# The first quarter of W_in at the head of the load queue, in a fused decay-attention and gated-MLP kernel

## The chip, the cores and the metric

The kernel runs on one core of a Trainium2 chip. The metric is the device time of one execution in microseconds (us), from repeated runs; a profiled execution, taken by the hardware profiler, gives the trace. Five engines work beside each other, each through its own instructions in order: PE (matrix products; its weight loads are shown apart as PEld), DVE and ACT (elementwise work, and copies out of PSUM, where PE writes), POOL (elementwise work in SBUF) and SP, which here only issues DMAs. The DMAs of a core share 16 DMA engines.

## The reference, cut to what matters

Two parts follow each other. First a linear attention with decay over 4 batches, 8 heads, 768 positions and head size 64, in blocks of 64 with a running state; then a gated MLP with a mixing over positions.

```python
for b in range(nb):                                     # blocks of 64 positions
    intra = np.einsum('bhic,bhjc->bhij', qb, kb) * Dmask[None]
    intra = np.einsum('bhij,bhjd->bhid', intra, vb)
    inter = np.einsum('bhid,bhde->bhie', qb * lam_pow[None], kv_state)
    out[:, :, sl] = intra + inter
    kv_state = lam_block[None, :, None, None] * kv_state + np.einsum('bhsd,bhse->bhde', kb_dec, vb)
...
h = np.maximum(x @ w_in, 0.0)                           # x: 4 x 768 x 512, w_in: 512 x 1024
u, v = h[..., :512], h[..., 512:]
v_n = (v - mu) / np.sqrt(var + 1e-06)
v_s = np.einsum('ts,bsd->btd', w_spatial, v_n) + b_spatial[None, :, None]
return (u * v_s) @ w_out
```

## The kernel before

The positions are worked in 12 steps of 256, three to a batch. A step loads 512 KB each of q, k and v (`load`, L193: per partition 8 heads of 2 positions, 512 bytes in a piece), multiplies q and k by powers of the decay and casts them to bf16 (`decay`, L328: `QM` and `KM`, on POOL or DVE), transposes them on PE (`TQ`, `TK`, L363), copies the transposes out of PSUM (`EQ`, `EK`), forms the scores on PE (`SC`, L393), masks them on DVE (`MK`, L398), and builds the output (`AV`, L456 and L465) and the state (`KP`, L422). The output, as `xT`, goes through W_in (`PV`, L490, the half v; `PU`, L541, the half u), then normalisation, the mixing over positions (`PW`, L567), the gate (`GM`, L573) and W_out (`PO`, L578).

Inputs arrive in float32 and pass through staging tiles. W_in comes in four quarters of 512 KB through `w_h` (L250): `WH.0` and `WH.1` are the two halves by rows of the columns for v, both in `wst_0`, with 2 KB in a piece; `WH.2` and `WH.3` are the columns for u, in `wst_1`. `CW.0` and `CW.1` cast the two row groups of `WH.0` to bf16, on POOL; `CW.2` and `CW.3` cast those of `WH.1`, on DVE. The first `PV` needs all four. There are three buffers each for q, k and v, so the loads of steps 0 to 2 wait for no buffer.

Before the first data, PE runs matmuls on a tile of ones (`FL`, L306) that no result uses.

Nothing schedules: a table written out by hand, `ORDER`, is the program. Each token names an operation, its arguments and, last, its engine (S is SP, P POOL, D DVE, A ACT, T PE); each engine runs its own tokens in the order of the table, and semaphores make it wait for data. `LK.n`, `LQ.n` and `LV.n` are the loads of step n, all on SP, one behind the other; so are the quarters of W_in and later the weights of the mixing (`WQ`, L271), W_out (`WP`, L280) and the stores (`ST`, L601).

Of the kernel before, what the change touches and what calls it, by code (L numbers as in the profile page):

```python
# [13 lines left out]


ORDER = """
lam.A BR.A tab.0.A LK.0.S LQ.0.S LV.0.S LQ.1.S LK.1.S LK.2.S LV.1.S LQ.2.S WH.0.S WH.1.S posk.P idn.P msk.P one.D
row.D FL.1.512.1.1.T FL.1.512.2.1.T FL.1.512.3.1.T LB.6.T FL.1.512.5.1.T FL.1.512.4.1.T FL.1.512.1.1.T FL.1.512.2.1.T
FL.1.512.3.1.T FL.1.512.4.1.T FL.1.512.1.1.T FL.1.512.5.1.T FL.1.512.2.1.T LN.6.A LL.D mkc.D LX.A QM.0.0.P TQ.0.0.1.T
KM.0.0.D KM.0.1.D QM.0.1.P TK.0.0.0.T TK.0.1.4.T TQ.0.1.3.T EK.0.0.0.D QM.1.0.D QM.1.1.D EQ.0.0.1.A EK.0.1.4.A VC.0.P  # L20
# [620 lines left out]
```

## Time and profile before

| | |
|---|---|
| time, median of 2 runs | 141.23 us (141.09 to 141.37) |
| time of the profiled execution | 141.1 us |
| its span, first to last instruction | 139.4 us |
| mean granted TensorE clock in the span | 0.983 |
| moved by DMA | 34.12 MB, mean 245 GB/s |
| read from and written to HBM | 24.38 MB, 6.29 MB |

The span is what the trace covers; the 1.7 us between it and the time lie around it. A share of busy time is a mean over the whole span, and the stages of a step have different limits, so the views are read by stretches of time. The time to landing in the list of DMA issues runs from the issue to the last byte, with whatever stands in front of it in the queue. Line numbers (L193 and so on) are those of the code above. An idle time in brackets is that of the engine just before the instruction, with what ended it.

### The profile page before, as it was taken

The numbers are of one execution on the slowest core, as the hardware profiler recorded it, in microseconds if no ns is written. First come the engines' busy times: TensorE is split into PE (matmuls) and PEld (weight loads), VectorE is DVE, ScalarE is ACT, GpSimd is POOL, SyncE is SP. The second block draws the span as 40 slices with busy tenths as digits, with TensorE's granted clock in tenths as the row PEclk, the third lists the DMA queues.
The fourth block names the chain that finished last, engine by engine and source line by source line (L and its number), as shares of the span: only waits on it lengthen the run. The fifth ranks groups of instructions, "written<-read, shape, count | busy, mean of one in ns | idle before, by whom it ended". The sixth has DMA issues, their size and how long they took to land.

```text
span 139.4 us, 4677 instructions
## 1 busy us (share of the span) xinstructions
PE 131.3 (94%) x1964; PEld 83.6 (60%) x1978; DVE 114.7 (82%) x235; ACT 76.2 (55%) x148; POOL 60.2 (43%) x70
## 2 busy tenths in 40 slices
PE   5889989999999999999999999999999999999990
PEld 2256755687766666658666466685565665756530
DVE  1549998999997989799788978999799699985470
ACT  3156468799733588659412177782313649790101
POOL 5168654942987458900942059907702000000000
PEclk9996899999999999999999999999999999999998
DMA  3999999999999899997941899999736540025285
GB/s 89 348 346 348 387 362 363 391 382 349 366 345 307 254 315 310 301 206 214 331 106 40 209 353 361 352 228 258 123 75 80 209 172 5 0 98 203 105 304 196
DMA packets 56729, 34.12 MB, mean 245 GB/s; under 512 B 13827, under 2 KB 51971, under 8 KB 56708
## 3 DMA queue, kind: packets, MB, share of 16 engines
q1 hardware_dynamic: 56560, 33.69, 83.5%
q8 instruction: 15, 0.25, 0.7%
q10 hardware_dynamic: 148, 0.13, 0.3%
q14 instruction: 6, 0.05, 0.1%
HBM read 24.38 MB, written 6.29 MB: 220 GB/s over the span
## 4 chain that ended last, share of the span: by engine, by line
PE 84%; DMA 4%; SPq 3%; DVE 3%; issue 2%; POOL 1%; ACT 0%; DVEq 0%; POOLq 0%
PE ps L567 23%; PE ps L541 15%; PE ps L490 15%; PE ps L578 14%; DMA k_in<-in_k_dram 4%; PE ps L393 4%; PE ps L465 4%; SPq L193 3%; PE ps L363 2%; PE ps L456 2%; PE ps L422 2%; POOL kc L328 1%; PE ps L553 1%; DVE qc L328 1%; PE ps L587 1%
## 5 line engine op out<-in xcount | busy, mean ns | idle before, releaser
L567 PE MATMUL ps<-wt_sb,vn 128*128 128x384 bf16 x192 | 33.1, 326 | 0.0
L398 DVE TENSOR_TENSOR a_sb<-ps,m 128x1024 bf16<-128x1024 f32 x24 | 28.6, 1215 | 2.3 <-PE ps L393 1.2
L328 POOL TENSOR_TENSOR kc<-k_in,lv 128x512 bf16<-128x512 f32 x22 | 22.5, 1042 | 14.7 <-PE ps L422 5.2
L567 PEld LDWEIGHTS <-vn 128*128 128x128 bf16 x192 | 18.4, 98 | 11.8
L541 PE MATMUL ps<-xT,win_sb 128*128 128x256 bf16 x192 | 23.5, 273 | 0.0
L328 POOL TENSOR_TENSOR qc<-q_in,lqn 128x512 bf16<-128x512 f32 x20 | 20.8, 1057 | 5.6 <-DMA q_in<-in_q_dram 5.5
L490 PE MATMUL ps<-win_sb,xT 128*128 128x512 bf16 x89 | 22.0, 379 | 0.5 <-issue 0.2
L578 PE MATMUL ps<-wout_sb,gT 128*128 128x512 bf16 x85 | 21.2, 380 | 0.4
L541 PEld LDWEIGHTS <-win_sb 128*128 128x128 bf16 x192 | 18.2, 98 | 3.9 <-DVE xT L180 0.2
L573 DVE TENSOR_TENSOR gT<-ps,uT 128x384 bf16<-128x384 f32 x32 | 16.7, 551 | 4.1 <-PE ps L567 4.0
L178 ACT ACTIVATE o_sb<-ps 128x512 f32<-128x512 f32 (+1 forms) x14 | 7.6, 565 | 16.6 <-PE ps L578 10.4
L505 DVE BATCH_NORM_STATS2 st<-vh 128x6 f32<-128x512 bf16 x24 | 16.3, 679 | 0.1
L182 POOL CAST vb<-v_in 128x1024 bf16<-128x1024 f32 (+1 forms) x10 | 9.9, 995 | 12.8 <-PE ps L465 6.7
L178 ACT ACTIVATE ps<-bsp 128x384 f32<-128x384 f32 x23 | 10.9, 487 | 7.2 <-DVE gT L573 5.2
L490 PEld LDWEIGHTS <-xT 128*128 128x128 bf16 x96 | 8.8, 98 | 9.8 <-ACT xT L178 1.5
L578 PEld LDWEIGHTS <-gT 128*128 128x128 bf16 x92 | 8.7, 98 | 9.3
L495 ACT ACTIVATE vh<-ps 128x512 bf16<-128x512 f32 x19 | 11.1, 597 | 5.8 <-PE ps L490 5.4
L178 ACT ACTIVATE xT<-ps 128x512 bf16<-128x512 f32 x20 | 11.1, 593 | 5.2 <-PE ps L465 4.4
L180 DVE COPY o_sb<-ps 128x512 f32<-128x512 f32 x11 | 7.6, 688 | 3.9 <-PE ps L578 3.3
L495 ACT ACTIVATE uT<-ps 128x512 bf16<-128x512 f32 x17 | 9.8, 591 | 1.4 <-PE ps L541 1.3
L393 PE MATMUL ps<-qT,kT 64*64 64x128 bf16 x384 | 10.1, 226 | 0.1
L465 PE MATMUL ps<-a_sb,vb 64*64 64x128 bf16 x384 | 10.2, 221 | 0.0
(78 smaller groups left out, 159.0 us busy)
## 6 DMA issues: line engine op xcount, KB each, us to landing
k_in<-in_k_dram SPq DMA_DIRECT2D x12, 512.0 KB, 6.3
q_in<-in_q_dram SPq DMA_DIRECT2D x12, 512.0 KB, 6.3
v_in<-in_v_dram SPq DMA_DIRECT2D x12, 512.0 KB, 6.7
out_dram<-o_sb SPq DMA_DIRECT2D x23, 256.0 KB, 2.4
wst<-in_moe_w_in_dram SPq DMA_DIRECT2D x4, 512.0 KB, 7.7
wst<-in_moe_w_spatial_dram SPq DMA_DIRECT2D x4, 384.0 KB, 5.5
wst<-in_moe_w_out_dram SPq DMA_DIRECT2D x1, 1024.0 KB
wss<-in_moe_w_spatial_dram SPq DMA_DIRECT2D x2, 384.0 KB, 6.0
```

The lines of the kernel that those rows point to most:

```text
L178: nc.scalar.activation(out=o, in_=i, func=AF.Copy)
L328: vec(e).tensor_tensor(out=dst[n % NCA][:, u].rearrange("p u m o d -> p o (u m) d"), in0=src[n % NIN].rearrange("p (o u) m d -> p o u m d" ...
L393: nc.tensor.matmul(out=pa[o][row(c), w, j], lhsT=kT[n % NTR][row(o), u, j, c * Q64:(c + 1) * Q64], rhs=qv(n, o, u, c), start=(w == 0 and j ...
L398: nc.vector.tensor_tensor(out=a_sb[n % NA][:, i].rearrange("p o w j x -> p o w (j x)"), in0=ps[:, b0:b1 + 1:b1 - b0].rearrange("p o (w y) ...
L465: nc.tensor.matmul(out=po[c ^ o][row(w), c, i], lhsT=vb[n % NCA][row(c), 4 * o + u, j, :], rhs=a[row(c), i, o, w, j, :], start=(r == 0 and ...
L490: nc.tensor.matmul(out=bank(b), lhsT=x[:, slot(c, g)], rhs=win_sb[:, g, DH:DFF], start=(g == 0), stop=(g == NCH - 1))
L495: nc.scalar.activation(out=o, in_=i, func=AF.Relu)
L505: nc.vector.bn_stats(out=st6[p2][:, t], in_=vh[p2][:, t])
L541: nc.tensor.matmul(out=pu[:, f2].rearrange("p (c x) -> p c x", c=2), lhsT=win_sb[:, g, f * P:(f + 1) * P], rhs=x[:, slot(0, g):slot(1, g) ...
L567: nc.tensor.matmul(out=bank(b)[:, 0:HW], lhsT=vn[bb % 2][:, s, f * P:(f + 1) * P], rhs=wt_sb[:, s, i * HW:(i + 1) * HW], start=False, stop ...
L573: nc.vector.tensor_tensor(out=gT[bb % 2][:, f, cols], in0=bank(b)[:, 0:HW], in1=uT[bb % 2][:, f, cols], op=ALU.mult)
L578: nc.tensor.matmul(out=bank(b), lhsT=gT[bb % 2][:, f, t * P:(t + 1) * P], rhs=wout_sb[:, f, :], start=(f == 0), stop=(f == NCH - 1))
```

## The change

One token of `ORDER` moves: `WH.0.S`, the load of the first quarter of W_in, from behind `LQ.2.S`, where it is the ninth load of SP's queue, to the front of it, ahead of `LK.0.S`.

```diff
-lam.A BR.A tab.0.A LK.0.S LQ.0.S LV.0.S LQ.1.S LK.1.S LK.2.S LV.1.S LQ.2.S WH.0.S WH.1.S posk.P idn.P msk.P one.D
+lam.A BR.A tab.0.A WH.0.S LK.0.S LQ.0.S LV.0.S LQ.1.S LK.1.S LK.2.S LV.1.S LQ.2.S WH.1.S posk.P idn.P msk.P one.D
```

The instructions of SP, at the head of its queue. In the names, the first digit is the buffer (here also the step), the last number is the tile's own; behind them stands the shape of the transfer:

```order
@@ -1,3 +1,4 @@
 L636 UNCONDITIONAL_BRANCH
+L250 DMA wst_0_141<-in_moe_w_in_dram 128x2x512
 L193 DMA k_in_0_93<-in_k_dram 128x8x128
 L193 DMA q_in_0_90<-in_q_dram 128x8x128
```

The quarter now stands ahead of k of step 0, and k, q and v of step 0 and all behind them move one place back. Further down the same queue, at the old place:

```order
 L193 DMA v_in_1_97<-in_v_dram 128x8x128
 L193 DMA q_in_2_92<-in_q_dram 128x8x128
-L250 DMA wst_0_141<-in_moe_w_in_dram 128x2x512 x2
+L250 DMA wst_0_141<-in_moe_w_in_dram 128x2x512
 L193 DMA v_in_2_98<-in_v_dram 128x8x128
 L250 DMA wst_1_142<-in_moe_w_in_dram 128x4x256
```

Of the two quarters that stood behind q of step 2 one is left there, and from it on every load has its old place. On PE, DVE, ACT and POOL the instructions and their order are the same before and after. On POOL, these rows use the loads of steps 0 to 2 and then the moved quarter (the last row):

```order
L328 TENSOR_TENSOR qc_0_101<-q_in_0_90,lqn_71 128x2x4x64 x2
L182 CAST vb_0_103<-v_in_0_96 128x1024
L328 TENSOR_TENSOR kc_1_100<-k_in_1_94,lv_70 128x2x4x64 x2
L328 TENSOR_TENSOR kc_0_99<-k_in_2_95,lv_70 128x2x4x64 x2
L182 CAST vb_1_104<-v_in_1_97 128x512
L328 TENSOR_TENSOR qc_0_101<-q_in_2_92,lqn_71 128x2x4x64
L182 CAST win_sb_84<-wst_0_141 128x512 x2
```

Neither their order nor their number moved; the casts of the quarter still stand behind the decay of q of step 2.

## The prediction

> **What bounds the kernel now.** I read the busy times first, then the same by stretches, then the chain of work that ended last, and for the start of that chain the order of time on single engines and on the DMA queue. The page's head, and a view of busy time in three stretches (columns: the stretch, its length, busy us and count of PE, PEld, DVE, ACT and POOL, then the granted TensorE clock, the DMA share and GB/s):
>
> ```profile
> span 139.4 us, 4677 instructions
> PE 131.3 (94%) x1964; PEld 83.6 (60%) x1978; DVE 114.7 (82%) x235; ACT 76.2 (55%) x148; POOL 60.2 (43%) x70
> 0.00:20.00 20.00, 16.40 (x315) 9.95 (x316) 13.37 (x26) 9.80 (x21) 12.18 (x21) 0.91 0.99 312
> 20.00:130.00 110.00, 109.09 (x1620) 70.78 (x1633) 97.13 (x204) 65.00 (x125) 48.00 (x49) 1.00 0.84 234
> ```
>
> From 20 us to 130 us PE shows no work in only 110.00 - 109.09 = 0.91 us. What starts late at 20 us therefore ends late: there is almost no idle time in which PE could catch up. Before 20 us PE is busy 16.40 us of 20, so something else sets the pace there. The chain in order of time (start, length, what) says what:
>
> ```profile
> 0.80 0.46 SPq L193
> ...
> 3.25 1.45 SPq L193
> 4.74 6.00 DMA k_in<-in_k_dram
> ...
> 10.87 2.05 POOL kc L328 x2
> ...
> 16.88 1.34 DVE qc L328
> ...
> 19.27 0.64 PE ps L393 x32
> 19.91 1.19 PE ps L490 x5
> ```
>
> The chain begins on the queue of loads: issues on SP, then the transfer of k of step 1, and only then engines. From 19.27 us it is PE. The order of time on DVE and POOL in that stage (in brackets the idle time before, and who ended it):
>
> ```profile
> 4.77 1.29 DVE L328 TENSOR_TENSOR kc<-k_in,lv 128x512 bf16<-128x512 f32 x2 [0.37 <-DMA k_in<-in_k_dram]
> 9.24 1.29 DVE L328 TENSOR_TENSOR qc<-q_in,lqn 128x512 bf16<-128x512 f32 x2 [0.74 <-DMA q_in<-in_q_dram]
> 10.45 2.46 DVE L398 TENSOR_TENSOR a_sb<-ps,m 128x1024 bf16<-128x1024 f32 x2
> 14.27 1.23 DVE L398 TENSOR_TENSOR a_sb<-ps,m 128x1024 bf16<-128x1024 f32 x1 [0.23 <-PE ps L393]
> 16.88 1.34 DVE L328 TENSOR_TENSOR qc<-q_in,lqn 128x512 bf16<-128x512 f32 x1
> 6.32 2.04 POOL L328 TENSOR_TENSOR qc<-q_in,lqn 128x512 bf16<-128x512 f32 x2 [3.34 <-DMA q_in<-in_q_dram]
> 10.87 4.05 POOL L328 TENSOR_TENSOR kc<-k_in,lv 128x512 bf16<-128x512 f32 x4 [1.53 <-DMA k_in<-in_k_dram]
> 16.63 1.04 POOL L328 TENSOR_TENSOR qc<-q_in,lqn 128x512 bf16<-128x512 f32 x1 [1.15 <-DMA q_in<-in_q_dram]
> 17.81 1.44 POOL L182 CAST win_sb<-wst 128x512 bf16<-128x512 f32 x2
> ```
>
> Five waits end with a load: k0 at 4.77, q0 at 6.32, q1 at 9.24, k1 at 10.87 and q2 at 16.63 us (the digit is the step). DVE, once it has q1, works with little pause up to 18.22 us. So the first stage is set by when the first eight loads land, and they land in the order in which SP issues them. Of that queue, the rate and the beginnings (the GB/s rows have 40 slices of the stretch named: first 0 to 4.7 us, then the totals of 4.7 to 6.5 and of 16.3 to 16.9 us, then the slices of 77.7 to 79.7 and of 108 to 110 us):
>
> ```profile
> GB/s 0 0 0 0 0 0 0 0 0 0 0 0 0 0 0 0 61 113 113 118 96 118 122 179 183 288 336 353 349 340 362 336 357 336 349 349 344 344 353 344
> DMA packets 1235, 0.62 MB, mean 347 GB/s; under 512 B 16, under 2 KB 1235, under 8 KB 1235
> DMA packets 121, 0.25 MB, mean 413 GB/s; under 512 B 0, under 2 KB 0, under 8 KB 121
> GB/s 0 31 51 82 51 41 41 51 92 20 20 31 41 82 102 113 133 174 195 123 123 123 143 143 225 266 297 297 338 338 348 328 338 389 369 328 348 338 348 328
> GB/s 0 0 0 0 287 205 451 410 369 492 287 492 492 287 451 410 369 205 41 0 0 0 0 0 0 0 0 0 0 0 0 0 0 0 0 0 0 0 0 0
> k_in<-in_k_dram SPq DMA_DIRECT2D x1, 512.0 KB, 3.9
> ```
>
> The q, k and v loads move in packets of 512 bytes, at 347 GB/s once under way: 512 KB (0.524 MB) take 1.51 us. W_in moves in packets of 2 KB, in the trace at 413 GB/s: a quarter, also 512 KB, takes 1.27 us. The first load does not begin at full rate.
>
> **The change part by part.** Removed: one DMA issue between q2 and the second quarter (rows of SP below). Added: the same DMA at the head of the queue. No instruction of PE, DVE, ACT or POOL changes or changes place.
>
> ```profile
> 9.21 1.45 SPq L193 DMA_DIRECT2D q_in<-in_q_dram  x1
> 10.70 2.00 SPq L250 DMA_DIRECT2D wst<-in_moe_w_in_dram  x2
> ```
>
> (1) What the eight loads lose. All of k0, q0, v0, q1, k1, k2, v1 and q2 now stand behind one more transfer of 512 KB. If it cost what a load costs, they would land 1.51 us later; at its own rate 1.27 us. But part of it falls into time that the queue now wastes. In the first row of GB/s the slices are 0.1175 us long; the eleven from 61 to 336 sum to 1727, where 347 in each would be 3817. The missing 2090 x 0.1175 us is 0.246 MB, which is 0.71 us at 347 GB/s. After a pause at 77.7 us a 512-byte load begins just as slowly (31 to 195 GB/s for the first 19 slices of 0.05 us), while a store with 2 KB packets, at 108 us, is at 287 in its first slice and about 400 at once. If the quarter began like that store and filled all of the slow beginning, the loads would lose 1.27 - 0.71 = 0.56 us. So the bounds are 0.56 and 1.51 us. The store's row is the nearest in packet size, though it is no load; and k0's own slow beginning would run mostly beside the quarter's transfer. I take 0.85 us, nearer the lower end, which is 0.42 of the 0.71 us won back.
>
> The Trainium skill, "DMA: Bandwidth & Descriptors", Specifications, gives 512 B as the smallest transfer for line rate. By that alone the quarter would cost what a load costs, 1.51 us, and the sum would be 142.6 us; the rows of 347 and 413 GB/s differ from it. That sum is rival B below.
>
> (2) What the later loads lose: nothing. The ninth place is empty now, so the second quarter stands behind the same bytes as before, and everything behind it too. Of the five waits listed none belongs to a load behind it.
>
> (3) What the quarter's early landing wins: nothing. It is used by the two casts on POOL at 17.81 us, which have no bracket: they begin when the decay of q2 (16.63 + 1.04 us) is done, and that waits for q2. POOL reaches them 0.85 us later than before. The other two casts, on DVE, also stand behind its work of this stage.
>
> (4) What of the 0.85 us is lost again before 19.27 us. On POOL nothing can be made up: its waits for k1 and q2 move with the loads. On DVE the stretch from q1 to 18.22 us has one wait for PE, 0.23 us at 14.27 us, which could shrink. A further reason for it stands in the clock (stretches as above):
>
> ```profile
> 8.40:11.82 3.42, 3.40 (x77) 1.96 (x78) 2.67 (x5) 2.03 (x5) 1.89 (x2) 1.00 1.15 346
> 11.82:15.23 3.41, 3.24 (x64) 2.53 (x62) 3.15 (x6) 2.26 (x5) 3.41 (x5) 0.50 1.14 355
> 15.23:18.64 3.41, 2.91 (x100) 2.05 (x100) 3.41 (x6) 1.72 (x4) 2.12 (x4) 1.00 1.09 382
> ```
>
> PE has half its clock from 11.82 to 15.23 us; work that slides past 15.23 us would run at full clock, if that stretch stays where it is. The gain is bounded by that wait: 0 to 0.23 us. I take 0, because the stretch may move with the load.
>
> (5) PE's pause. The filler matmuls on ones need no load and end when they did; the first transposes come later:
>
> ```profile
> 3.44 2.86 PE L306 MATMUL ps<-ones 128*128 128x512 bf16 x9
> 7.42 0.40 PE L363 MATMUL ps<-ident,qc 128*128 128x128 bf16 x4 [1.12 <-POOL qc L328]
> ```
>
> The pause of 1.12 us grows to 1.97 us. Nothing is lost by the pause itself beyond (1).
>
> Sum: the profiled execution took 141.1 us, its span 139.4 us and 1.7 us around it. 141.1 + 0.85 (1) + 0 (2) + 0 (3) - 0 (4) = 141.95, said as 142.0 us. The median of the two runs, 141.23 us, is 0.13 us above that execution, well inside what I can price.
>
> **The rivals.** A: the forecast, a delay of about 0.6 to 1.1 us that passes through whole, 141.7 to 142.2 us. For it: five waits on loads, a stage that ends on PE at 19.27 us, and 0.91 us of idle PE in the 110 us behind.
>
> B: the quarter costs a full slot, 1.2 to 1.5 us: 142.3 to 142.6 us. For it: the slow beginning may belong to the first load from a queue at rest, of whatever packet; the 2 KB row is a store. Against it: packets that are four times as large ought to bring four times the bytes at the same count.
>
> C: the delay is hidden or made up, 141.0 to 141.4 us. For it: 0.56 us less the 0.23 us of DVE's wait is 0.33 us, and a little of the 0.91 us of idle PE could go too. Against it: DVE and POOL both hang on loads before 17 us.
>
> D, the other side of 2%: TensorE's clock stays at half for one stretch more, 15.23 to 18.64 us, since PE has less work in the time before. In that stretch it is busy 2.91 us at full clock and would need up to 2.91 us more, which gives 141.95 + 2.91 = 144.9 us at most. It decides (over 2%, that is over 144.05 us) from 2.1 us of these 2.91 that reach the end. Against it: DVE is busy all of that stretch (3.41 of 3.41 us), so it hides much of a slower PE, and the half-clock stretch itself was left after 3.41 us with PE busy 3.24.
>
> The Trainium skill, "TensorE: Matmul & The Clock Gate", Part 1, has the clock halved after an idle window of about 3.4 us. By that rule a pause of 1.97 us changes nothing and D would give 141.95 us like A. The trace agrees in the length, 3.41 us, but not in the cause: the half clock came after a stretch in which PE was busy 3.40 of 3.42 us. So D keeps a chance.
>
> **How the numbers follow.** A 0.55, B 0.20, C 0.14, D 0.11 (half of it over 2%). The time is A's, 142.0 us. The range must leave out no more than 2 in 10: from 141.2, within C (half of C left out, 0.07), to 143.0 us, which holds B and the smaller part of D (about 0.08 left out). A alone has 141.7 to 142.2. About 2% is what a measurement of this kernel can tell from no change, so a slowdown of 0.6% counts as the same. Faster by over 2% would need a gain, and no part shows one: 0.01. Slower by over 2% is half of D: 0.06. The same: 0.93.
>
> **What would show it.** In the trace after: DVE's first decay of k0 at about 5.6 us instead of 4.77, q1's at about 10.1 instead of 9.24, POOL's k1 at 11.7 instead of 10.87, q2's at 17.5 instead of 16.63; the casts of W_in on POOL without a wait, at 18.7; the scores of step 2 on PE at about 20.1 instead of 19.27. In the first GB/s slices no row near 113. From 20 us on every stage the same length. B shows as 1.2 us or more at the same places; C as a shift at 5 us that is gone at 20 us; D as a clock of 0.50 behind 15.23 us. The prediction is wrong if the first loads land no later, or if a stage behind 20 us changes its length by more than some tenths of a us.

## The result, and the profile after

The changed kernel takes 145.46 us (median of 2 runs, 145.33 to 145.58) where the kernel before takes 141.23: the ratio is 1.0266, 95% interval 1.0208 to 1.0324. A second measurement, of six runs beside seventeen of the kernel before, gave 146.16 us against 141.52, ratio 1.0327 (1.0283 to 1.0372). It is slower by some 4.2 to 4.6 us, and lies above the predicted range. One slow run, of e10 below (145.96 us), is left out of the medians and ratios.

The head of the page after, and busy time by stretches (columns as before):

```profile
span 143.9 us, 4677 instructions
PE 134.6 (94%) x1964; PEld 85.4 (59%) x1978; DVE 114.2 (79%) x235; ACT 76.2 (53%) x148; POOL 60.3 (42%) x70
0.00:20.00 20.00, 15.57 (x163) 8.34 (x164) 8.29 (x17) 6.80 (x14) 11.38 (x21) 0.76 0.96 283
20.00:130.00 110.00, 108.84 (x1745) 71.47 (x1759) 99.62 (x208) 67.85 (x131) 48.96 (x50) 1.00 0.84 233
```

PE has done 163 matmuls by 20 us where it had done 315, and DVE 8.29 us of work instead of 13.37; the mean clock of that stretch is 0.76 instead of 0.91. Behind it nothing changed. The first product with W_in, in the kernel before and then after:

```profile
19.84 3.63 PE L490 MATMUL ps<-win_sb,xT 128*128 128x512 bf16 x15
```

```profile
24.29 3.63 PE L490 MATMUL ps<-win_sb,xT 128*128 128x512 bf16 x15
```

From its start to the end of the span it is 139.4 - 19.84 = 119.56 us before and 143.9 - 24.29 = 119.61 us after. The whole difference, 4.45 us, is there at this product. How it comes about stands in the order of time on DVE and POOL after:

```profile
7.31 1.29 DVE L328 TENSOR_TENSOR kc<-k_in,lv 128x512 bf16<-128x512 f32 x2 [2.91 <-DMA k_in<-in_k_dram]
11.81 1.29 DVE L328 TENSOR_TENSOR qc<-q_in,lqn 128x512 bf16<-128x512 f32 x2 [0.77 <-DMA q_in<-in_q_dram]
13.02 1.22 DVE L398 TENSOR_TENSOR a_sb<-ps,m 128x1024 bf16<-128x1024 f32 x1
16.55 1.23 DVE L398 TENSOR_TENSOR a_sb<-ps,m 128x1024 bf16<-128x1024 f32 x1 [2.31 <-PE ps L393]
19.27 1.23 DVE L398 TENSOR_TENSOR a_sb<-ps,m 128x1024 bf16<-128x1024 f32 x1 [0.49 <-PE ps L393]
21.87 0.68 DVE L328 TENSOR_TENSOR qc<-q_in,lqn 128x512 bf16<-128x512 f32 x1
24.47 2.36 DVE L398 TENSOR_TENSOR a_sb<-ps,m 128x1024 bf16<-128x1024 f32 x2
8.86 2.04 POOL L328 TENSOR_TENSOR qc<-q_in,lqn 128x512 bf16<-128x512 f32 x2 [5.89 <-DMA q_in<-in_q_dram]
13.71 4.04 POOL L328 TENSOR_TENSOR kc<-k_in,lv 128x512 bf16<-128x512 f32 x4 [1.83 <-DMA k_in<-in_k_dram]
18.27 1.04 POOL L328 TENSOR_TENSOR qc<-q_in,lqn 128x512 bf16<-128x512 f32 x1
19.25 1.16 POOL L182 CAST win_sb<-wst 128x512 bf16<-128x512 f32 x2
```

Two parts can be read off. First, the loads: k0, q0 and q1 are used 2.54, 2.54 and 2.57 us later (4.77, 6.32 and 9.24 us before). Second, a longer stage: from q1's use to the masks of step 2 (the last DVE row; 20.14 us before) it is 12.66 us instead of 10.90, so 1.76 us more. In it DVE waits for scores of PE, 2.31 and 0.49 us, where before it waited 0.23. These waits grew by 2.57 us, more than the stage; DVE's other rows became shorter, above all its decay of q2, 0.68 us instead of 1.34. POOL reaches its own part of q2 at 18.27 us and, unlike before (16.63), does not wait for the load there. Why PE is late, in stretches of its clock, and in its order of time (the bias matmuls of L292 were 0.91 us a pair before):

```profile
7.03:10.44 3.41, 0.76 (x10) 0.49 (x10) 1.29 (x2) 0.05 (x1) 1.58 (x2) 1.00 1.13 337
10.44:20.68 10.24, 9.97 (x149) 6.40 (x147) 6.50 (x11) 4.81 (x10) 8.14 (x10) 0.50 1.06 323
```

```profile
3.44 3.87 PE L306 MATMUL ps<-ones 128*128 128x512 bf16 x9
9.96 0.40 PE L363 MATMUL ps<-ident,qc 128*128 128x128 bf16 x4 [2.65 <-POOL qc L328]
...
12.06 1.64 PE L292 MATMUL ps<-bsp,one_row 1*128 1x384 f32 x2
13.63 0.64 PE L422 MATMUL ps<-vb,kc 64*64 64x64 bf16 x32
14.21 1.64 PE L292 MATMUL ps<-bsp,one_row 1*128 1x384 f32 x2
15.78 0.64 PE L393 MATMUL ps<-qT,kT 64*64 64x128 bf16 x16
```

PE's pause is 2.65 us instead of 1.12, and its clock is halved from 10.44 to 20.68 us, 10.24 us instead of 3.41. The two pairs of bias matmuls stand in PE's order between the first and the second half of step 0's scores; at half clock they take 1.64 us each instead of 0.91, and the second half of the scores, for which DVE's second mask waits, starts only at 15.78. The chain of waits now runs through them:

```profile
1.82 6.89 DMA q_in<-in_q_dram
...
12.13 1.57 PE ps L292 x2
13.70 0.57 PE ps L422 x26
14.28 1.57 PE ps L292 x2
15.85 0.57 PE ps L393 x14
```

And the slow beginning of the queue did not go; GB/s in slices of 0.1175 us from 0 to 4.7 us:

```profile
GB/s 0 0 0 0 0 0 0 0 0 0 0 0 0 0 0 0 139 52 70 17 105 401 314 296 227 139 209 192 244 261 366 292 314 218 183 140 209 301 296 327
DMA packets 476, 0.62 MB, mean 133 GB/s; under 512 B 15, under 2 KB 224, under 8 KB 476
```

In 4.7 us 0.62 MB were moved where the kernel before had moved 0.73 MB. With W_in at the head the queue is slower, not faster, and slow until about 4.5 us.

### The profile page after: what moved, and what is told of

The parts are those of the page before. It is cut to its first block, busy times and chain, and to the rows that moved or that the text cites. A ratio compares the mean times of both kernels' runs of the same rounds, so it can differ in the third digit from the quotient of the medians.

```text
span 143.9 us, 4677 instructions
## 1 busy us (share of the span) xinstructions
PE 134.6 (94%) x1964; PEld 85.4 (59%) x1978; DVE 114.2 (79%) x235; ACT 76.2 (53%) x148; POOL 60.3 (42%) x70
## 4 chain that ended last, share of the span: by engine, by line
PE 82%; DVE 6%; DMA 5%; issue 2%; ACT 1%; POOL 1%; SPq 1%; DVEq 0%; POOLq 0%
PE ps L567 22%; PE ps L541 15%; PE ps L578 14%; PE ps L490 12%; DMA q_in<-in_q_dram 5%; PE ps L393 5%; PE ps L363 3%; PE ps L465 3%; DVE a_sb L398 2%; PE ps L456 2%; PE ps L292 2%; PE ps L422 2%; PE ps L553 1%; DVE win_sb L180 1%; DVE s_sb L437 1%
## 5 line engine op out<-in xcount | busy, mean ns | idle before, releaser
L398 DVE TENSOR_TENSOR a_sb<-ps,m 128x1024 bf16<-128x1024 f32 x24 | 28.6, 1217 | 4.7 <-PE ps L393 3.7
L393 PE MATMUL ps<-qT,kT 64*64 64x128 bf16 x384 | 10.6, 234 | 0.3 <-ACT kT L178 0.3
L178 ACT ACTIVATE qT<-ps 128x512 bf16<-128x512 bf16 (+1 forms) x7 | 5.4, 776 | 9.9 <-PE ps L363 9.9
```

Of the source, the lines that this page charges most:

```text
L178: nc.scalar.activation(out=o, in_=i, func=AF.Copy)
L393: nc.tensor.matmul(out=pa[o][row(c), w, j], lhsT=kT[n % NTR][row(o), u, j, c * Q64:(c + 1) * Q64], rhs=qv(n, o, u, c), start=(w == 0 and j ...
L398: nc.vector.tensor_tensor(out=a_sb[n % NA][:, i].rearrange("p o w j x -> p o w (j x)"), in0=ps[:, b0:b1 + 1:b1 - b0].rearrange("p o (w y) ...
```

## The experiments

The theory after the first result had two parts. L: the loads come 2.5 us late, and that passes to the end. C: PE's half-clock stretch is longer because PE pauses longer, and that costs the other 1.8 us, through DVE's wait for scores. The rivals are that the clock costs nothing, that its stretches are chance, or that the quarter's bytes disturb something else.

This table holds, for each run, when k0 is first used, PE's pause ahead of its first transpose, how long the granted clock is 0.50 in the first 25 us, the stage from q1's use to the masks of step 2, and the time (the median, with the ratio to the kernel before where it was repeated; otherwise one time, beside 141.06 us for the kernel before in e5 to e8 and 141.26 in e13 and e14). All but the times come from one trace each. Between traces with the same loads, k0's first use varies by 0.2 to 0.3 us (4.77 to 4.96 us with k0 first, 7.01 to 7.31 with the quarter first), so smaller differences mean nothing.

| run | k0 used | pause | half clock | stage | time |
|---|---|---|---|---|---|
| before | 4.77 | 1.12 | 3.41 | 10.90 | 141.23 |
| changed | 7.31 | 2.65 | 10.24 | 12.66 | 145.46, 1.0266 |
| e1 longer filler | 7.15 | 0.26 | 3.41 | 11.29 | 144.03, 1.0195 (1.0155 to 1.0235) |
| e2 wait only | 7.08 | 3.45 | 13.65 | 13.43 | 145.68, 1.0322 (1.027 to 1.0373) |
| e3 quarter second | 4.96 | 3.35 | 13.65 | 13.26 | 146.56, 1.0357 (1.0278 to 1.0435) |
| e4 no filler | 4.94 | 4.94 | to about 19.6 us | 13.38 | 143.73, 1.0179 (1.0131 to 1.0227) |
| e5 q2 first | 6.52 | 1.92 | 10.24 | 12.88 | 144.79 |
| e6 512-byte pieces | 6.49 | 1.75 | 10.24 | 12.77 | 144.59 |
| e7 half a quarter | 5.65 | 1.18 | 6.83 | 11.99 | 142.76 |
| e8 quarter fifth | 4.80 | 0.43 | 6.83 | 13.51 | 144.18 |
| e9 changed again | 7.17 | 2.60 | 10.24 | 14.26 | 146.16, 1.0327 (1.0283 to 1.0372) |
| e10 changed, bias early | 7.01 | 1.89 | 10.24 | 11.57 | 144.16, 1.0185 (1.0138 to 1.0232) |
| e11 before, bias early | 4.94 | none | 3.41 | 10.89 | 141.66, 1.001 (0.9981 to 1.0039) |
| e12 wait, longer filler | 7.08 | 0.64 | none | 10.59 | 143.36, 1.0136 (1.0095 to 1.0177) |
| e13 W_out first | 6.08 | 1.32 | 6.83 | 11.71 | 143.01 |
| e14 two halves | 8.25 | 4.62 | 13.65 | 15.29 | 148.51 |
| e15 before, longer filler | 4.94 | 0.19 | 6.83 | 11.22 | 141.89, 1.0023 (0.9995 to 1.005) |

In e4 the trace has no record of the clock ahead of 19.6 us; the half clock is read from its bias matmuls (1.64 us a pair).

**e1.** More matmuls on ones behind the filler of the changed kernel:

```diff
-FL.1.512.2.1.T LN.6.A
+FL.1.512.2.1.T FL.10.512.5.1.T LN.6.A
```

> The changed kernel with ten more matmuls on ones behind the filler, so that PE's pause before its first transpose (2.65 us in the changed kernel) is nearly filled. The loads are as in the changed kernel: k0 is used at about 7.3 us. Theory L+C (of the 4.4 us, about 2.5 are late loads and about 1.9 are TensorE's half clock, which lasted 10.24 us instead of 3.41 because of the pause): the half-clock stretch gets shorter or goes, and the time falls to 143.2 to 144.0 us. Rival L (all of it is the late loads): 145.2 to 145.7 us whatever the clock does. Rival P (the length of the half-clock stretch is chance of that run and not an effect of the pause): the stretch may be of any length, without relation to the pause.

The loads came as late, and the half-clock stretch fell to 3.41 us; the stage is 11.29 us, and 144.03 us lies just over the upper edge of what L+C expected, clear of rival L. The interval of its ratio lies below that of the changed kernel's second measurement; with that of the first, of two runs, it overlaps.

**e2.** The order of the loads of the kernel before, held back by a memset on POOL behind its masks:

```diff
-LK.0.S LQ.0.S
...
-posk.P idn.P msk.P
+posk.P idn.P msk.P HL.0.0.P LK.0.S LQ.0.S
```

> The kernel before, its order of loads untouched, but the first load waits until POOL has built its masks (about 3.0 us), so that all loads start about 2.2 us later with nothing put ahead of them. Theory L+C: k0 is used near 7.0 us, PE pauses about 2.4 us longer than before, the half-clock stretch is long again, and the time is 144.8 to 145.6 us: the bytes of the quarter do not matter, only how late k0 and the rest come. Rival B (the quarter's transfer itself disturbs the later ones): 143.0 to 143.6 us, 2.2 us above the kernel before.

145.68 us: as slow as the changed kernel (slightly above the band), with nothing put ahead of the loads. So their lateness, with the long half clock that follows, is enough; the quarter's bytes are not needed for it. Its two rows:

```profile
7.08 1.29 DVE L328 TENSOR_TENSOR kc<-k_in,lv 128x512 bf16<-128x512 f32 x2 [2.68 <-DMA k_in<-in_k_dram]
8.29:21.93 13.64, 11.97 (x196) 8.42 (x200) 7.82 (x14) 5.39 (x11) 9.80 (x11) 0.50 1.13 360
```

**e3.** The quarter behind k0:

```diff
-WH.0.S LK.0.S LQ.0.S
+LK.0.S WH.0.S LQ.0.S
```

> The quarter stands second, behind k0, and all else is as in the changed kernel. If the quarter is dear because it is the first transfer from rest (slow first packets), k0 is used at 4.8 us as before and q0 and those behind it come 1.2 to 1.5 us later than before, not 2.5; the time is then 142.3 to 143.3 us, or up to 144.5 us if the half-clock stretch becomes long. If 2 KB packets are dear at any place at this time, q0 comes 2.5 us later than before (8.8 us) and the time is near 145 us.

k0 was in time, but q0 was used at 8.55 us and q1 at 11.65, 2.2 and 2.4 us later than before, near the expectation that 2 KB pieces are dear at any place this early. That the first transfer from rest is slow is therefore not the whole explanation. The time, 146.56 us, was above both expectations.

**e4.** No filler at all (twelve `FL` tokens out). They compute nothing that is used.

> The kernel before without any filler matmul (they compute nothing that is used); the loads are untouched, so k0 is used at 4.8 us and q1 at 9.2 us as before. It measures the clock by itself. Theory L+C: PE is at half clock from its first transposes to well beyond 12 us, and the time rises by 1 to 2.5 us, to 142.2 to 143.7 us, with DVE waiting for PE before its masks. Rival L: 141.0 to 141.6 us, since the loads set the stage.

The loads were as early as before, and the time rose by 2.4 us (143.73 against 141.37), to the upper edge of the band, so rival L falls: with the loads in time, PE's half clock costs that. DVE, in the rows of its second and third mask, waits as in the changed kernel (L397 is here what L398 is there):

```profile
14.47 1.22 DVE L397 TENSOR_TENSOR a_sb<-ps,m 128x1024 bf16<-128x1024 f32 x1 [2.61 <-PE ps L392]
17.19 1.23 DVE L397 TENSOR_TENSOR a_sb<-ps,m 128x1024 bf16<-128x1024 f32 x1 [0.49 <-PE ps L392]
```

**e5.** Another load of 512 KB at the head:

```diff
-LK.0.S LQ.0.S LV.0.S LQ.1.S LK.1.S LK.2.S LV.1.S LQ.2.S
+LQ.2.S LK.0.S LQ.0.S LV.0.S LQ.1.S LK.1.S LK.2.S LV.1.S
```

> The kernel before with the eighth load, q2 (512 KB in 512-byte pieces), moved to the head instead of the quarter of W_in. Read by when k0 is first used (4.77 us before, 7.31 us in the changed kernel). Theory S (any extra 512 KB at the head costs one slot of 1.5 us, and the rest of the 2.5 us is particular to the quarter): 6.2 to 6.4 us. Theory H (the first transfer from rest pays about 1 us more, whatever it is): 7.2 to 7.4 us.

6.52 us: 1.75 us more than before, between the two theories and nearer to S. A plain load at the head costs its slot and a little more, not 2.5 us.

**e6.** The quarter in pieces of 512 bytes, in two transfers, into a padded part of a tile that is free at that time:

```diff
...
+        if j == 0:
+            for h in range(2):
+                nc.sync.dma_start(out=wpad[:, h, :, 0:P], in_=moe_w_in.rearrange(
+                    "(g p) (c x) -> p g c x", p=P, x=P)[:, h, DH // P:DFF // P])
+            return
...
```

> The changed kernel, but the quarter comes in two transfers of 256 KB in 512-byte pieces (into a padded tile, so that pieces cannot be joined). If the 2 KB pieces are what is dear early in the kernel, k0 is used at 6.2 to 6.5 us. If W_in itself is dear (first touch of that tensor), at 7.2 us or later.

6.49 us, like e5. The same bytes of W_in in small pieces cost 1.72 us; in 2 KB pieces the changed kernel lost 2.54. So small pieces are here the cheaper ones. The tile that receives them and the split in two also differ from the changed kernel; in e14 a split alone makes k0 later, not earlier.

**e7.** Half of the quarter (one row group) at the head, the other half at the old place:

```diff
-WH.0.S LK.0.S
+WF.0.S LK.0.S
...
-LQ.2.S WH.1.S
+LQ.2.S WF.1.S WH.1.S
```

> The changed kernel with only the first 256 KB of the quarter at the head, in one transfer of 2 KB pieces; the other 256 KB stand at the old place. If the loss of 2.5 us is in proportion to the bytes, k0 is used at 6.0 us (half of 2.54 above 4.77); if about 1 us of it is a fixed price of the first transfer, at 6.5 us.

5.65 us, a loss of 0.88: less than either expectation, and less than half of 2.54, though more than the 0.63 us that 256 KB take at 413 GB/s.

**e8.** The quarter fifth, ahead of k1:

```diff
-WH.0.S LK.0.S LQ.0.S LV.0.S LQ.1.S LK.1.S
+LK.0.S LQ.0.S LV.0.S LQ.1.S WH.0.S LK.1.S
```

> The quarter stands fifth, behind q1 and ahead of k1; all else as in the changed kernel. k0, q0, v0 and q1 are used as before (q1 at 9.24 us). If the 2 KB pieces are slow only while the queue is still filling, k1 is used at 12.1 to 12.4 us (10.87 before, plus 1.27 to 1.5); if they are slow there too, at about 13.3 us. PE's pause is as before, so the half-clock stretch should last 3.4 us, and the time is 142.4 to 143 us.

k0 to q1 were in time, and k1 was used 1.80 us late (12.67 against 10.87), between the two figures. (The bracket of that row names a copy of q on ACT; before, the same row started at 10.87 us, ahead of that copy at 11.93, so it does not need it, and the wait is put down to the load.) The quarter itself was not slow here: from 8.4 to 10.0 us, while its packets ran, the queue moved 391 GB/s in the mean. The half-clock stretch was 6.83 us and not 3.4, and the time 144.18 us, above the band: the expectation missed that a late k1 also leaves PE idle (1.57 us at 13.76 us), although the first pause was short.

**e9.** The changed kernel again.

> The changed kernel as it is, for a second profile and more runs. If the pieces of the loss are steady, k0 is used at 7.2 to 7.4 us, PE pauses for 2.5 to 2.8 us, the half-clock stretch is 10.24 us or a whole number of 3.41 us near it, and the time is 145.2 to 145.8 us. If the slow 2 KB pieces of the quarter or the place of the clock's stretches are chance of a run, k0 comes anywhere from 6.3 to 7.4 us, or the stretch differs, and the runs spread over more than 1 us.

The late loads, the pause and the half-clock stretch came back almost the same; the times spread more than expected (145.36 to 146.88). The stage is 1.60 us longer than in the first trace, and not through PE: DVE waits for the scores as long as there (2.31 and 0.49 us), but its decay of q2 took 1.43 us instead of 0.68 and its two casts of W_in 1.59 instead of 0.75. The first product with W_in starts only 0.50 us later (24.79), so not all of that reaches the end.

**e10.** The changed kernel with the bias matmuls and copies put into the pause:

```diff
-FL.1.512.2.1.T LN.6.A LL.D mkc.D LX.A QM.0.0.P
+FL.1.512.2.1.T LN.6.A LL.D mkc.D LX.A BB.1.2.T BB.0.5.T BE.1.2.A BE.0.5.A QM.0.0.P
...
-SC.0.0.0.1.T EQ.0.1.3.A BB.1.2.T KP.0.6.T BB.0.3.T BE.1.2.A BE.0.3.A SC.0.1.4.5.T
+SC.0.0.0.1.T EQ.0.1.3.A KP.0.6.T SC.0.1.4.5.T
```

> The changed kernel with the four matmuls and two copies that spread the bias over the partitions put into PE's pause, behind the filler, instead of between the scores of step 0. It tests through which instructions the half clock is paid: at half clock these matmuls stood 3.28 us in front of PE's next scores, and DVE's second mask waited 2.31 us. The loads are unchanged (k0 at 7.2 to 7.4 us). Theory L+C: DVE's wait falls under 1 us and the time is 143.3 to 144.3 us. If the bias matmuls are not the place: 145 us or more.

```profile
12.71 2.35 DVE L398 TENSOR_TENSOR a_sb<-ps,m 128x1024 bf16<-128x1024 f32 x2
16.50 1.23 DVE L398 TENSOR_TENSOR a_sb<-ps,m 128x1024 bf16<-128x1024 f32 x1 [0.23 <-PE ps L393]
8.36:18.59 10.23, 8.28 (x164) 6.73 (x168) 7.17 (x12) 4.13 (x9) 7.62 (x8) 0.50 1.13 345
```

The half-clock stretch is as long as in e9 (10.23 us), but DVE's two first masks now follow each other without a wait, the third waits 0.23 us, and the time is 144.16 us, 2.00 us below e9 of the same measurement; the intervals of the two ratios don't touch. So the long half clock is paid for mainly in one place: the bias matmuls in front of step 0's second scores.

**e11.** The same move in the kernel before (with three filler matmuls fewer).

> The kernel before with the same move of the bias matmuls, into its own pause of 1.12 us (three of the filler matmuls left out for them). Loads untouched. If the loads and DVE set its stage, 0 to 0.4 us less than the kernel before; if PE's half clock from 11.8 us costs it more than DVE's wait of 0.23 us showed, 0.5 to 1 us less.

No difference (1.001, 0.9981 to 1.0039). With early loads DVE has no wait there that could go.

**e12.** e2 with a longer filler (`FL.12.512.5.1.T` at the place shown in e1).

> The kernel with the loads held back until about 3 us and nothing put ahead of them, with twelve more filler matmuls against PE's longer pause. It is late loads without a long pause: k0 used near 7.1 us, 2.3 us later than before. Theory L+C: 143.4 to 144.2 us, against 145.68 us without these matmuls; if the pause is not what lengthens the half-clock stretch, 145 us or more.

```profile
11.54 1.29 DVE L328 TENSOR_TENSOR qc<-q_in,lqn 128x512 bf16<-128x512 f32 x2 [0.77 <-DMA q_in<-in_q_dram]
12.76 2.42 DVE L398 TENSOR_TENSOR a_sb<-ps,m 128x1024 bf16<-128x1024 f32 x2
22.13 2.34 DVE L398 TENSOR_TENSOR a_sb<-ps,m 128x1024 bf16<-128x1024 f32 x2
5.32:21.84 16.52, 14.07 (x319) 8.68 (x316) 12.01 (x21) 7.59 (x17) 10.11 (x11) 1.00 1.13 358
```

Loads as late as in e2, the clock full throughout, and 143.36 us, just under the lower edge of the band: 2.3 us less than e2. This is the delay of the loads by itself. It is 2.31 us at k0 and costs 143.36 - 141.52 = 1.84 us.

**e13.** The kernel before with 512 KB of W_out added at the head in 2 KB pieces; the content is not used, and the quarter of W_in stays at its old place.

```diff
...
+    def w_j(e):
+        nc.sync.dma_start(out=wst[0][:, 0:2], in_=moe_w_out.rearrange("(t p) f -> p t f", p=P)[:, 0:2])
...
```

> The kernel before with an additional transfer at the head: 512 KB of W_out, 2 KB pieces over two row groups, into the staging tile (its content is not used; the quarter of W_in overwrites it at its old place). If 2 KB pieces in such a transfer are dear early whatever the tensor, k0 is used at 7.0 to 7.3 us, as in the changed kernel. If it is W_in with its row pitch of 4 KB, at 6.0 to 6.5 us.

6.08 us, a loss of 1.31 us. Pieces of 2 KB as such are not dear: from W_out the transfer costs what the rate of 413 GB/s gives (1.27 us). So the rest of the 2.54 us comes with W_in in 2 KB pieces: neither their size alone (here) nor the tensor alone (e6) brings it.

**e14.** The quarter at the head as two transfers of one row group each (`WF.0.S WF.1.S` in place of `WH.0.S`).

> The changed kernel with the quarter at the head as two transfers of 256 KB, one row group each, 2 KB pieces. If the form of the one transfer over two row groups is what is dear, k0 is used at 6.3 to 6.6 us (twice the 0.88 us of e7 above 4.77 us); if the second half meets the slow pieces anyway, at 7.0 to 7.3 us.

```profile
wst<-in_moe_w_in_dram SPq DMA_DIRECT2D x2, 256.0 KB, 2.9
...
GB/s 164 293 410 375 345 398 339 278 193 94 85 85 120 170 214 246 278 278 301 310 293 296 296 328 322 316 336 331 339 325 293 313 336 363 336 357 345 331 301 164
```

8.25 us, worse than in one transfer, which neither guess foresaw. The first row is from the list of DMA issues (the median from issue to landing), the second has GB/s in slices of 0.175 us from 2 to 9 us. The two halves landed 2.9 us after their issue, at up to 410 GB/s; then the queue fell to 85 GB/s, and was below 200 from 3.4 to 4.4 us. That is a second slow beginning, behind the quarter, where the first 512-byte load starts. So the quarter does not cover k0's slow beginning; here it even stands ahead of it in full. Over the whole queue, though, nothing more is lost than in the changed kernel: to 6 us it moved 1.04 MB, there 1.05.

**e15.** The kernel before with `FL.4.512.5.1.T` added to its filler.

> The kernel before with four more filler matmuls in its pause of 1.12 us, loads untouched. If its half-clock stretch from 11.8 us goes and costs it 0.4 us (the part of 2.3 us that e12 did not lose): 140.9 to 141.2 us where the kernel before has 141.4. If DVE and the loads hide it: no difference, within 0.2 us.

No gain (1.0023, 0.9995 to 1.005), and its half-clock stretch was longer, not shorter. It cost nothing: it began behind the bias matmuls, which took 0.91 us a pair, and DVE waited 0.23 us for the scores, as before. So it was in e7 and e8 too, also with 6.83 us; in e13, with the same length, the second pair fell into it (1.64 us) and DVE waited 1.17 us. In these traces it matters more whether the half clock meets those matmuls than how long it lasts. No version here beats the kernel before.

## Why the prediction was wrong, point by point

**What bounds the kernel** was right: the first loads set the stage before 20 us, and behind it nothing can be made up (119.56 and 119.61 us).

**(1), what the eight loads lose, was mis-sized.** The term was 0.85 us between bounds of 0.56 and 1.51; it measured 2.54 us (2.24 to 2.54 in four runs with the quarter at the head). Two assumptions fell. The slow beginning was taken to belong to 512-byte packets, so that the quarter would fill part of 0.71 us: but even W_out's 2 KB pieces lost their whole slot, 1.31 us, and q2 at the head lost 1.75. In this rival B was right: with 2 KB pieces first, nothing of the slow beginning was won back. The store taken as nearest row was no guide to a load. (The row at 77.7 us was also misread, without consequence: its first 19 slices with traffic go from 20 to 195 GB/s, not from 31.) And the rate of W_in's pieces was read at 16 us (413 GB/s, 1.27 us); at the head and in second place the same transfer delayed the load behind it by more (2.54 us at k0, and 2.2 us at q0 in e3). In fifth place, with the queue at 391 GB/s in the mean, k1 was still used 1.80 us late (e8). The bound of 1.51 us was no bound, since nothing in the trace before showed this transfer early. And k0's own slow beginning did not run beside the quarter's transfer: e14 shows it behind the quarter, and the changed kernel has a dip to 140 GB/s at 4.1 us. That the loads lose more behind W_in's quarter than behind as many bytes of W_out is shown; why is not. W_in's row pitch of 4 KB, or where it lies in memory, would fit e13, but the first half in e7, with 0.88 us, suits no simple rule.

The totals of the queue show how the 2.54 us divide. To 6 us it had moved 1.18 MB before and 1.05 MB after; the 0.13 MB are some 0.4 us at 347 GB/s. The slot of 512 KB at that rate is 1.51 us. That makes 1.9 us; the other 0.6 us are not in the queue's total. What fits them is that the quarter ends unevenly. From 4.2 to 5.2 us, behind W_in's quarter (first row) and behind W_out in e13 (second row):

```profile
DMA packets 504, 0.29 MB, mean 294 GB/s; under 512 B 12, under 2 KB 477, under 8 KB 504
DMA packets 682, 0.35 MB, mean 349 GB/s; under 512 B 0, under 2 KB 682, under 8 KB 682
```

In the changed kernel 27 packets of 2 KB still ran while hundreds of smaller ones already did; behind W_out none was left. A load can be used only when its last packet has landed, so k0 may have waited for its parts behind the late ones. The traces kept here do not name the DMA engine of a packet, so this is not shown.

The Trainium skill, "DMA: Bandwidth & Descriptors", Specifications, takes 512 B as enough for line rate. The traces agree only in part: once under way, 512-byte packets moved at 347 GB/s and those of 2 KB at 413; at the head, 512-byte pieces cost 1.72 to 1.75 us, and from W_in they were cheaper than pieces of 2 KB.

**(2)** was wrong in size, without consequence: the loads behind the ninth place were said to lose nothing, but v of step 2 was issued at 15.19 us instead of 12.75, and POOL waited 1.78 us for it at 22 us. Nothing on the chain waits for that. **(3)** was right: the casts of the quarter stand on POOL without a wait (19.25 us), and its early landing wins nothing.

**(4) was wrong in sign.** It allowed a gain of up to 0.23 us from the clock. The stage from q1 to the masks of step 2 became 1.76 us longer.

**(5) was the second failing step:** "Nothing is lost by the pause itself beyond (1)". Where the pause was filled (e1, e12), the half-clock stretch was 3.41 us or nothing; where 1.75 us or more of it was left, 10.24 to 13.65 us. That costs some 2 us: e2 less e12 is 2.3 us, e9 less e10 2.00 us, and the stage of the first result grew by 1.76. Its sentence that the filler ends when it did was wrong too: the same matmuls ended at 7.31 us instead of 6.30 (3.44 + 3.87 against 3.44 + 2.86), so the pause grew by 1.53 us and not by the whole 2.54.

**Rival D** had the right mechanism and the wrong size. It saw one more stretch of half clock and trusted DVE to hide it, because DVE was busy from 15.23 to 18.64 us. The stretch became three times as long and started earlier, and DVE's cover ended at 13.02 + 1.22 us, where it waited 2.31 us for scores. The prediction looked at busy shares there and not at what stood in PE's order ahead of those scores: 3.28 us of bias matmuls at half clock.

The Trainium skill, "TensorE: Matmul & The Clock Gate", Part 1, describes free-running windows of about 3.4 us. The traces agree: the stretches are 3.41, 6.83, 10.24 and 13.65 us long, and begin at different times from run to run. The same part of the Trainium skill has the clock halved after at least one idle window; here less was enough: pauses of 1.75 to 2.65 us, in a stretch with sparse work around them, were followed by 10.24 us at half clock.

**Together:** 2.57 us (q1 late) + 1.76 us (longer stage) = 4.33 us at the masks of step 2, and 145.46 - 141.23 = 4.23 us in the time. For most other runs the same sum gives the time within 0.5 us (e12: 2.30 - 0.31 = 1.99, measured 1.84; e5: 1.77 + 1.98 = 3.75, measured 3.73); e14 is off by 0.6 us and e9 by 1.15, the latter with the longer rows of DVE told above. So the stage holds more than PE's clock, and the sum is a reading of single traces, not a proof.

What stays open, beside W_in: the length of the half-clock stretch after short pauses. With pauses under 0.7 us it was none, 3.41 or 6.83 us. These stretches begin at other times in each run, so chance has a part in them, and no run was made that fixes their start. The pause has a part of chance as well: in e2, e3 and e14, with the longest pauses after a filler, the filler ended by 6.3 us, in the changed kernel and e9 at 7.2 to 7.3.

## What to carry to other kernels

When a change delays the first data, price two things: the delay, and what the idle matrix engine's clock does to the stage that follows; look in that engine's order for work that stands ahead of what others wait for, since its price can nearly double (here from 0.91 to 1.64 us a pair). A transfer's rate read deep in a full queue need not be what the same transfer costs at the queue's head; without a row of that transfer at that place, the upper bound should be left wide. Work that needs no late data, such as the bias here, is safest in the pause that the late data leave.

## What was unexpected of the hardware

The same 512 KB at the head of the queue delayed k0 by 1.31 us from W_out in 2 KB pieces, 1.72 us from W_in in 512-byte pieces, 2.54 us from W_in in 2 KB pieces and 3.48 us from W_in in two transfers of 2 KB pieces. And PE's half-clock stretches came in steps of 3.41 us, longer after longer pauses: 3.41 to 6.83 us after 1.12 to 1.32 us, 10.24 us after 1.75 to 2.65 us, 13.65 us after 3.35 to 4.62 us; but 6.83 us also came after pauses of only 0.19 and 0.43 us, so the pause alone does not set them.
